# The first loads of a convolution's input on another queue, a longer pause behind them, and new shares for its stages

## The chip, the cores and the metric

The kernel runs on one core of a Trainium2 chip. The metric is device time in microseconds (us) of one execution, smaller is better; the time given for a kernel is the median of its runs. A core has five engines that each work through a queue of their own in order: TensorE (PE, matrix products; PEld is its loading of weights), VectorE (DVE), ScalarE (ACT), GpSimd (POOL) and SyncE (SP). SP computes nothing here: it issues DMAs. ACT and POOL can issue DMAs too, and an instruction of theirs that stands behind a DMA issue waits for that issue. Engines wait for each other by semaphores.

## The reference

Two branches over a sequence of S = 2048 rows of D = 576 numbers are summed with the input. Branch A is a short causal convolution of `k` (four taps), a product with `v`, a long causal convolution per channel (by FFT in the reference), and a gate. Branch B is a dense network with a ReLU.

```python
xn = _layernorm(x, axis=-1)
# A, with q = xn:
for t in range(ks):                                   # ks = 4
    k_shift = k_shift + k_pad[:, t:t + S, :] * shift_k[:, ks - 1 - t][None, None, :]
kv = k_shift * v
y = irfft(rfft(kv) * rfft(ssm_k)) + kv * ssm_D
A = q * y
# B:
B = maximum(xn @ w1, 0) @ w2                          # w1: 576 x 4608, w2: 4608 x 576
return x + A + B
```

## The kernel before

**Precision.** Matrix products are done with operands split into a high and a low part; a product is the sum of three: high by high, high by low, low by high. ACT makes the high part by a copy, DVE or POOL the low part by a subtraction.

**The network (FFN).** Its 4608 hidden columns are worked in 18 pairs of 2 x 128, and rows in four blocks of 512, two blocks a half: first half (blocks 0 and 1) over all 18 pairs, then second half (blocks 2 and 3), which uses a product scheme with fewer multiplications (`quad`, L515). A visit is one pair with one block. `mm1` (L539) makes two tiles `psh` of hidden values in PSUM, fourteen matmuls each. `relu` then has ACT write the high part `hh` (L521) and DVE the low part `ll` (L522). A `unit` (L602) multiplies `hh` and `ll` with a half of `w2`, twelve matmuls for two pairs, into a tile `pso`, which DVE adds to the accumulator `acc` (L606 or L610). There are three buffers for `pso` and two banks for `psh`. Weights come by SP (`load_w1`, L421 and L423; `load_w2`, L430) and are split by ACT (L439, L501) and POOL (L410).

**The long convolution.** `conv` is a generator of small steps that are strewn among the FFN's. Its stages: FK transforms the kernel `ssm_k` (matmuls L652, stores `zk` L718); FX makes the four taps, the product with `v` and the transform of the result (matmuls L652, stores `zx` L809); FM does the middle transform, the product with FK's result and the middle inverse (matmuls L848, loads `zk` and `zx`, stores `zy`); FO does the last inverse transform, gates and adds (matmuls L989, L990). In FX, `load(t)` (L733) loads a tile of `k` and of `v`, for t below 0 the shifted rows of `k` (L744, L745), all through `move` (L156) or directly; `sk` holds the four taps' factors (L729), each broadcast to 128 partitions. `tap` (L754, L757, L758) and `gate` (L763) are DVE's; `split` (L773, L776, L777) stacks the halves, and two DMAs on SP move a half of the result, `c`, into each stack `xs` (L780), on which the transform's matmuls work.

**Rows of the second half.** A second generator, `later_xT`, prepares the blocks 2 and 3 beside all this: it loads rows, normalizes them, stores them to DRAM as `nrm` (L325), loads them back in pieces, `rows` from `nrm` (L333), transposes (L338), splits, and stores the operands (`kept_t` L349, `kept_xr` L394).

**What sets the order.** The FFN's code calls `tick(cost)` with the columns of each few matmuls. `tick` adds `rate * cost` to a balance and lets `conv` take its next step when the balance is not negative. A step that yields a positive number costs that many units (`W_FK`, `W_FX`, `W_FM`, `W_FO`, with `N_...` steps each). A step that yields a negative number holds the stream until that many columns of the FFN have passed; `PAUSE` is 16,000 columns. `rate` is set so that the whole stream, `FFT_TOTAL` units and `PAUSES` pauses, fits into `SHARE` of the FFN's columns. A scheduler then puts the recorded instructions into each engine's queue; `here()` keeps a step's instructions behind the FFN's latest ones. The wait of a DMA on one of eight rotating semaphores keeps some eight DMAs of these two queues under way at a time.

```python
rate = FFT_TOTAL / (SHARE * FFN_TOTAL - PAUSES * PAUSE - START)
```

Of the kernel before, what the change touches and what calls it, by code (L numbers as in the profile page):

```python
# [17 lines left out]
P = 128  # L18
S = 2048
D = 576  # L20
# [3 lines left out]
NH = D // 2  # L24
# [24 lines left out]
PAUSE = 16000  # L49
# [2 lines left out]


N_FK, N_FX, N_FM, N_FO = 4 * T, 4 * T, 6 * NG, 4 * T
W_FK, W_FX, W_FM, W_FO = 1.25, 4.8, 1.72, 2.15
Q = 32
KB = 3
KT_GAP = 2000
PAUSES = 4 * NH // Q // KB * KT_GAP / PAUSE + 11
FFT_TOTAL = N_FK * W_FK + N_FX * W_FX + N_FM * W_FM + N_FO * W_FO  # L60
W_QUAD = sum(W_STAGE)
FFN_TOTAL = NPAIR * HB * (W_PLAIN + W_QUAD + 2 * 4 * W_UNIT)
# [47 lines left out]
def h3_ffn_kernel(ctx: ExitStack, tc, x, k, v, shift_k, ssm_k, ssm_D, w1, w2, fwd, inv, mid, out):  # L110
    nc = tc.nc
# [37 lines left out]
    def halves(u):  # L149

        return slice(u * A1, (u + 1) * A1), slice((1 - u) * A1, (2 - u) * A1)

    def move(tile_, rows, t, store=False, queues=(nc.sync, nc.sync)):
        for u in range(U):
            a, b = tile_[halves(u)[0]], rows[u, :, t]
            queues[u].dma_start(*((b, a) if store else (a, b)))  # L156
# [41 lines left out]
    def f32(t):  # L198
        return t.bitcast(F32)
# [437 lines left out]
    def load_const(pool, src, name):  # L637
        w = pool.tile([P, 2, P], F32R, tag="wt", name=name, bufs=3)
        nc.gpsimd.dma_start(w, src)
        return w  # L640
# [7 lines left out]
    def first(w, stk, z, u):  # L648

        ps = fft_psum()  # L650
        for n in range(2):
            nc.tensor.matmul(ps[:, :NH], w[:, n, :], stk, start=n == 0, stop=n == 1)  # L652
        nc.scalar.activation(z, ps[:, :NH], AF.Copy)  # L653

    @contextmanager
    def here():


        with tc.issue_after(done["acc"].ins), tc.issue_after(done["act"].ins):
            yield  # L660

    def conv():
# [4 lines left out]
        with tc.tile_pool(name="fk", bufs=2) as fp:  # L667
# [44 lines left out]
            for n, t2 in enumerate(order):  # L712
                stk, nxt = nxt, []
                u, t = divmod(t2, T)
# [11 lines left out]
        with tc.tile_pool(name="fx", bufs=2) as fp:  # L726
            sk = fp.tile([P, KS, D], F32, tag="sk", name="sk", bufs=1)
            for j in range(KS):
                nc.scalar.dma_start(sk[:, j, :], shift_k[j:j + 1, :].to_broadcast([P, D]))  # L729
            win, gates, mats, sums, stks = {}, {}, {}, {}, {}  # L730

            def load(t):
                win[t] = fp.tile([P, D], F32, tag="k", name=f"k{t}", bufs=KS + 1)  # L733
                queue = nc.scalar if t < 2 else nc.sync
                if t >= 0:
                    move(win[t], k, t, queues=(queue, queue))
                    gates[t] = fp.tile([P, D], F32, tag="v", name=f"v{t}")
                    move(gates[t], v, t, queues=(queue, queue))
                    if t == 0:
                        for n in range(3):  # L740
                            mats[n] = load_const(fp, fwd[n // U][:, n % U], f"wx{n}")
                else:
                    nc.vector.memset(win[t][0:1, :], 0.0)
                    queue.dma_start(win[t][1:A1, :], k[1, 0:A1 - 1, T + t, :])  # L744
                    queue.dma_start(win[t][A1:, :], k[0, :, T + t, :])  # L745

            def tap(t, n):

                if t >= T:
                    return  # L750
                with here():
                    if n == 0:
                        sums[t] = fp.tile([P, D], F32, tag="c", name=f"c{t}")
                        nc.vector.tensor_tensor(sums[t], win[t], sk[:, 0, :], OP.mult)  # L754
                    else:
                        e = fp.tile([P, D], F32, tag="e", name=f"e{t}_{n}")
                        nc.vector.tensor_tensor(e, win[t - n], sk[:, n, :], OP.mult)  # L757
                        nc.vector.tensor_tensor(sums[t], sums[t], e, OP.add)  # L758

            def gate(t):  # L760
                if t < T:
                    with here():
                        nc.vector.tensor_tensor(sums[t], sums[t], gates[t], OP.mult)  # L763

            def split(t):

                if t < T:
                    hi = fp.tile([P, D], F32R, tag="e", name=f"h{t}")
                    lo = sums[t].bitcast(F32R)
                    for u in range(U):  # L770
                        stks[t, u] = fp.tile([P, D], F32R, tag="stk", name=f"xs{t}_{u}", bufs=3)
                    with here():
                        nc.scalar.activation(hi, sums[t], AF.Copy)  # L773
                        for u in range(U):
                            own = halves(u)[0]
                            nc.scalar.activation(stks[t, u][own], sums[t][own], AF.Copy)  # L776
                        nc.vector.tensor_tensor(lo, sums[t], hi, OP.subtract)  # L777
                    for u in range(U):
                        own, other = halves(u)
                        nc.sync.dma_start(f32(stks[t, u])[other], sums[t][own])  # L780

            with here():
                for t in (0, *range(-1, -KS, -1), 1):
                    load(t)
            yield -3 * PAUSE
            for n in range(KS):
                tap(0, n)
                yield -PAUSE / 8
            gate(0)
            yield -PAUSE / 8  # L790
            split(0)
            yield -PAUSE / 8
            for n in range(KS):
                tap(1, n)
                yield -PAUSE / 4
            for t in range(T):
                if t + 2 < T:
                    load(t + 2)

                side = (((gate, t + 1),), ((split, t + 1),),  # L800
                        (), ((tap, t + 2, 0),),
                        ((tap, t + 2, 1),), (),
                        ((tap, t + 2, 2),), ((tap, t + 2, 3),))
                for u in range(U):
                    for h in range(2):
                        cols = slice(h * NH, (h + 1) * NH)
                        z = fp.tile([P, NH], F32, tag="z", name=f"zx_{t}_{u}_{h}", bufs=3)
                        first(mats[U * t + u], stks[t, u][:, cols], z, u)
                        nc.sync.dma_start(zx[:, T * u + t, cols], z)  # L809
                        for part in range(2):  # L810
                            for what, *args in side[4 * u + 2 * h + part]:
                                what(*args)
                            yield W_FX / 2
                    n = U * t + u + 3
                    if n < U * T:
                        mats[n] = load_const(fp, fwd[n // U][:, n % U], f"wx{n}")
# [186 lines left out]


    stream = conv()
    clock = {"ffn": 0.0, "conv": 0.0, "until": START, "done": False}
    rate = FFT_TOTAL / (SHARE * FFN_TOTAL - PAUSES * PAUSE - START)

# [161 lines left out]
```

## Time and profile before

| | us |
|---|---|
| median of 3 runs (lowest, highest) | 1087.82 (1085.5, 1089.77) |
| the profiled execution's own time | 1086.3 |
| its span, first to last instruction | 1084.5 |
| mean granted TensorE clock | 0.992 of full |
| DVE busy | 745.1 |
| ACT busy | 549.2 |
| POOL busy | 392.5 |
| DMA, mean rate | 189 GB/s |

The span is what all views count from: 0 is the first instruction. Busy times of different engines overlap. The views used are windows (busy time of each engine in a stretch of the span), the timeline (instructions in order, with the idle time before one and what ended it in brackets), the waits (who waited for whom, in total, how often, longest) and the rows of the page. In timelines, ACTq and SPq are the issuing of DMAs by ACT and SP. Buffer numbers are left out there, so `hh` stands for every `hh` tile.

### The profile page before, as it was taken

The page shows a single profiled execution, that of the slowest core. Times are in us where ns is not written, and L with a number is a line of the kernel's source. Part 1 is how long each engine was busy: PE and PEld are TensorE (multiplying, and loading weights), DVE is VectorE, ACT ScalarE, POOL GpSimd, SP SyncE. Part 2 cuts the span into 40 slices and gives each one's busy share as a digit, 9 for nine tenths or more (in the row PEclk, how much of TensorE's full clock was granted, in tenths as well). Part 3 has the DMA queues.
Part 4 walks back from the last instruction along what each step waited for, and adds up shares of the span by engine and source line. Part 5 has one row for each costly group of instructions (what it writes and reads, how often), then busy time and mean ns, then how long its engine had stood idle before and what let it go on. Part 6 is the DMA issues. An engine that isn't in the chain of part 4 may idle for free.

```text
span 1084.5 us, 19961 instructions
## 1 busy us (share of the span) xinstructions
PE 1058.6 (98%) x7145; PEld 992.8 (92%) x7145; DVE 745.1 (69%) x1310; ACT 549.2 (51%) x1201; POOL 392.5 (36%) x395
## 2 busy tenths in 40 slices
PE   8999999979899999999999999999999999999998
PEld 5799999969799999999899999999999999999998
DVE  5438788768787866652387677677767876576664
ACT  4225565524444333332567577776776765444431
POOL 4122333313323333333334334344433444444551
PEclk9999999989999999999999999999999999999999
DMA  7665776577886685444878455555555644997854
GB/s 194 142 158 175 184 208 197 166 204 202 229 241 192 189 266 150 126 116 148 274 217 242 148 170 166 167 179 156 165 155 157 189 136 131 320 304 235 259 174 110
DMA packets 156303, 204.45 MB, mean 189 GB/s; under 512 B 32845, under 2 KB 122703, under 8 KB 155180
## 3 DMA queue, kind: packets, MB, share of 16 engines
q1 hardware_dynamic: 141636, 185.76, 58.0%
q0 software_dynamic: 12576, 13.44, 5.2%
q10 hardware_dynamic: 1992, 3.98, 1.4%
q8 instruction: 56, 0.92, 0.4%
q14 instruction: 43, 0.35, 0.1%
HBM read 133.92 MB, written 55.05 MB: 174 GB/s over the span
## 4 chain that ended last, share of the span: by engine, by line
PE 88%; DMA 6%; DVE 2%; issue 1%; ACT 1%; POOL 0%; ACTq 0%; SPq 0%; POOLq 0%; DVEq 0%
PE pso L602 39%; PE psh L539 20%; PE psb L515 12%; PE psf L848 7%; PE psa L515 6%; PE psf L652 3%; DMA r<-in_w 3%; DMA ztk<-zk 1%; DMA zo<-zy 1%; PE psf L989 1%; PE psf L990 1%; DMA zy<-vo 1%; DMA xs<-c 1%; DMA k<-in_k 0%; DVE acc L606 0%
## 5 line engine op out<-in xcount | busy, mean ns | idle before, releaser
L602 PE MATMUL pso<-w,hh 128*128 128x288 f32 x2304 | 469.5, 296 | 6.1 <-ACT hh L521 4.7
L602 PEld LDWEIGHTS pso<-w,hh 128*128 128x128 f32 x2304 | 373.4, 188 | 15.1 <-ACT hh L521 5.8
L602 PE MATMUL pso<-w,ll 128*128 128x288 f32 x1152 | 329.0, 296 | 2.8 <-DVE ll L522 2.8
L410 POOL TENSOR_TENSOR g<-r,g 128x256 fp32r<-128x256 f32 (+2 forms) x145 | 163.3, 1132 | 397.8 <-ACT g L439 348.7
L539 PE MATMUL psh<-b,g 128*128 128x512 f32 x864 | 221.9, 400 | 0.5 <-ACT b L219 0.5
L602 PEld LDWEIGHTS pso<-w,ll 128*128 128x128 f32 x1152 | 213.0, 188 | 4.3 <-DVE ll L522 3.4
L539 PEld LDWEIGHTS psh<-b,g 128*128 128x128 f32 x864 | 159.8, 191 | 32.0 <-ACT b L219 1.0
L610 DVE TENSOR_TENSOR acc<-pso,acc 128x288 f32<-128x288 f32 x224 | 98.7, 450 | 74.9 <-PE pso L602 73.9
L410 POOL TENSOR_TENSOR w<-r,w 128x576 fp32r<-128x576 f32 x72 | 117.6, 1633 | 58.5 <-ACT w L501 58.4
L521 ACT ACTIVATE hh<-psh 128x512 fp32r<-128x512 f32 x72 | 42.9, 596 | 132.2 <-PE psh L539 115.2
L522 DVE SCALAR_TENSOR_TENSOR ll<-psh,hh 128x512 fp32r<-128x512 f32 x72 | 49.2, 684 | 73.6 <-ACT hh L521 73.5
L439 ACT ACTIVATE g<-r 128x256 fp32r<-128x256 f32 (+2 forms) x145 | 76.7, 542 | 35.3 <-DMA r<-in_w 27.6
L515 PE MATMUL psb<-t,g 128*128 128x256 f32 x648 | 93.9, 280 | 0.3 <-DVE psa L570 0.3
L515 PEld LDWEIGHTS psb<-t,g 128*128 128x128 f32 x648 | 84.9, 188 | 0.8 <-DVE psa L570 0.5
L468 POOL TENSOR_TENSOR r<-r 128x256 f32<-128x256 f32 x72 | 59.5, 846 | 52.1 <-DMA r<-in_w 50.6
L515 PE MATMUL psa<-b,g 128*128 128x256 f32 x432 | 62.7, 281 | 0.3 <-ACT psa L566 0.3
L515 PE MATMUL psb<-b,g 128*128 128x256 f32 x432 | 57.5, 281 | 0.0
L515 PEld LDWEIGHTS psa<-b,g 128*128 128x128 f32 x432 | 56.4, 188 | 0.5 <-ACT psa L566 0.5
L515 PEld LDWEIGHTS psb<-b,g 128*128 128x128 f32 x432 | 54.3, 188 | 0.0
L606 DVE SCALAR_TENSOR_TENSOR acc<-pso,rstd,acc 128x288 f32<-128x288 f32 x80 | 40.5, 511 | 18.9 <-PE pso L602 18.3
L839 DVE TENSOR_TENSOR lok<-ztk,hik 128x576 fp32r<-128x576 f32 x32 | 35.3, 1105 | 19.9 <-ACT hik L838 19.6
L653 ACT ACTIVATE zx<-psf 128x288 f32<-128x288 f32 x64 | 25.2, 405 | 46.4 <-issue 19.4
(137 smaller groups left out, 1665.9 us busy)
## 6 DMA issues: line engine op xcount, KB each, us to landing
r<-in_w SPq DMA_DIRECT2D x72, 288.0 KB, 4.0
zy<-vo SPq DMA_DIRECT2D x64, 288.0 KB, 3.3
zo<-zy SPq DMA_DIRECT2D x32, 576.0 KB, 5.9
r<-in_w SPq DMA_DIRECT2D x35, 512.0 KB, 4.8
zk<-zk SPq DMA_DIRECT2D x64, 144.0 KB, 2.2
zx<-zx SPq DMA_DIRECT2D x64, 144.0 KB, 2.6
ztk<-zk SPq DMA_DIRECT2D x32, 288.0 KB, 4.1
ztx<-zx SPq DMA_DIRECT2D x32, 288.0 KB, 3.1
```

The lines of the kernel that those rows point to most:

```text
L410: return nc.gpsimd.tensor_tensor(dst, src, hi, OP.subtract)
L439: nc.scalar.activation(hi, src, AF.Copy)
L468: nc.gpsimd.tensor_tensor(dst, a, b, op)
L515: nc.tensor.matmul(ps, a, m, start=start and i == 0, stop=i == len(seq) - 1, skip_group_check=not start)
L521: done["act"] = nc.scalar.activation(hh, ps, AF.Relu)
L522: lows.append(nc.vector.scalar_tensor_tensor(ll, ps, 0.0, hh, op0=OP.max, op1=OP.subtract))
L539: nc.tensor.matmul(ps, a, m, start=i == 0, stop=i == len(seq) - 1)
L602: nc.tensor.matmul(ps[:, :NH], a, m, start=c == 0, stop=c == len(seq) - 1)
L606: done["acc"] = nc.vector.scalar_tensor_tensor(acc[t][:, dc], ps[:, :NH], rstd[:, t:t + 1], acc[t][:, dc], op0=OP.mult, op1=OP.add)
L610: done["acc"] = nc.vector.tensor_tensor(acc[t][:, dc], ps[:, :NH], acc[t][:, dc], OP.add)
L839: nc.vector.tensor_tensor(lo, raw[name, g], hi, OP.subtract)
L848: nc.tensor.matmul(ps[:, :NH], a, m[:, cols], start=n == 0, stop=n == 2)
```

## The change

Two edits are in the code of stage FX. The sources of the first loads (`sk`, and `load` of tiles 0, −1, −2, −3 and 1) go to SP's queue, where they had gone to ACT's. The pause behind these loads is five units and was three, and the one behind each of the first tile's four taps is a quarter of a unit and was an eighth. Three numbers of the pacing follow: `PAUSES` grows by 2.5, the weight of a step of FM falls from 1.72 to 1.58, that of FO rises from 2.15 to 2.35.

```diff
-W_FK, W_FX, W_FM, W_FO = 1.25, 4.8, 1.72, 2.15
+W_FK, W_FX, W_FM, W_FO = 1.25, 4.8, 1.58, 2.35
-PAUSES = 4 * NH // Q // KB * KT_GAP / PAUSE + 11
+PAUSES = 4 * NH // Q // KB * KT_GAP / PAUSE + 13.5
             for j in range(KS):
-                nc.scalar.dma_start(sk[:, j, :], shift_k[j:j + 1, :].to_broadcast([P, D]))
+                nc.sync.dma_start(sk[:, j, :], shift_k[j:j + 1, :].to_broadcast([P, D]))
...
-                queue = nc.scalar if t < 2 else nc.sync
+                queue = nc.sync
...
                 for t in (0, *range(-1, -KS, -1), 1):
                     load(t)
-            yield -3 * PAUSE
+            yield -5 * PAUSE
             for n in range(KS):
                 tap(0, n)
-                yield -PAUSE / 8
+                yield -PAUSE / 4
```

The numbers move instructions on all engines from here on. Three places matter.

**The start of FX, on ACT and SP.** Names carry the tile's numbers: `hh7_1_1` is of pair 7, block 1, second tile. ACT before, from the first load of the factors on:

```order
L729 DMA sk_2156<-in_shift_k 128x576 x4
L156 DMA k0_2161<-in_k 64x576 x2
L156 DMA v0_2164<-in_v 64x576 x2
L744 DMA k-1_2173<-in_k 63x576
L745 DMA k-1_2173<-in_k 64x576
L744 DMA k-2_2177<-in_k 63x576
L745 DMA k-2_2177<-in_k 64x576
L744 DMA k-3_2181<-in_k 63x576
L745 DMA k-3_2181<-in_k 64x576
L156 DMA k1_2185<-in_k 64x576 x2
L156 DMA v1_2188<-in_v 64x576 x2
L521 ACTIVATE hh7_1_1_2640<-psh7_1_1_2625 128x512
```

ACT at the same place now, from the instruction on that stood just ahead of these:

```order
L347 ACTIVATE area2_680<-area2_680 128x256
L521 ACTIVATE hh7_1_1_2622<-psh7_1_1_2607 128x512
L392 ACTIVATE rows2_679<-rows2_679 64x512
L521 ACTIVATE hh7_0_0_2677<-psh7_0_0_2661 128x512
L439 ACTIVATE g8_1_2704<-r1_8_2518 128x512
```

SP before, behind the last store of FK:

```order
L718 DMA zk_86<-zk31_1_2140 128x288
L349 DMA kept_t_92<-area2_680 128x2x256
L430 DMA r2_8_0_2602<-in_w2 128x2x288
L156 DMA k2_2714<-in_k 64x576 x2
L394 DMA kept_xr_93<-rows2_679 128x512
L430 DMA r2_8_1_2734<-in_w2 128x2x288
```

SP now, behind the same store:

```order
L729 DMA sk_2156<-in_shift_k 128x576 x4
L156 DMA k0_2161<-in_k 64x576 x2
L156 DMA v0_2164<-in_v 64x576 x2
L744 DMA k-1_2173<-in_k 63x576
L745 DMA k-1_2173<-in_k 64x576
L744 DMA k-2_2177<-in_k 63x576
L745 DMA k-2_2177<-in_k 64x576
L744 DMA k-3_2181<-in_k 63x576
L745 DMA k-3_2181<-in_k 64x576
L156 DMA k1_2185<-in_k 64x576 x2
L156 DMA v1_2188<-in_v 64x576 x2
L430 DMA r2_8_0_2584<-in_w2 128x2x288
```

The 18 loads left ACT; on SP they stand ahead of the weights `r2_8_0` and of the store `kept_t`, which had no load ahead of them.

**The first taps, on DVE.** Before, from the first tap's product `c0` on:

```order
L754 TENSOR_TENSOR c0_2396<-k0_2161,sk_2156 128x576
L757 TENSOR_TENSOR e0_1_2422<-k-1_2173,sk_2156 128x576
L757 TENSOR_TENSOR e0_2_2441<-k-2_2177,sk_2156 128x576
L758 TENSOR_TENSOR c0_2396<-c0_2396,e0_1_2422 128x576
L758 TENSOR_TENSOR c0_2396<-c0_2396,e0_2_2441 128x576
L757 TENSOR_TENSOR e0_3_2479<-k-3_2181,sk_2156 128x576
L754 TENSOR_TENSOR c1_2576<-k1_2185,sk_2156 128x576
L522 SCALAR_TENSOR_TENSOR ll7_1_1_2641<-psh7_1_1_2625,hh7_1_1_2640 128x512
L393 TENSOR_TENSOR rows2_679<-rows2_679 64x512
L522 SCALAR_TENSOR_TENSOR ll7_0_0_2698<-psh7_0_0_2679,hh7_0_0_2697 128x512
L758 TENSOR_TENSOR c0_2396<-c0_2396,e0_3_2479 128x576
L610 TENSOR_TENSOR acc4_222<-pso6_4_0_2701,acc4_222 128x288
```

DVE now, from the low part `ll7_1_1` on:

```order
L522 SCALAR_TENSOR_TENSOR ll7_1_1_2623<-psh7_1_1_2607,hh7_1_1_2622 128x512
L606 SCALAR_TENSOR_TENSOR acc2_99<-pso5_2_1_2626,rstd_84,acc2_99 128x288
L338 STREAM_TRANSPOSE rows2_679<-rows2_679 64x512
L606 SCALAR_TENSOR_TENSOR acc2_99<-pso5_3_1_2647,rstd_84,acc2_99 128x288
L754 TENSOR_TENSOR c0_2533<-k0_2161,sk_2156 128x576
L393 TENSOR_TENSOR rows2_679<-rows2_679 64x512
L757 TENSOR_TENSOR e0_1_2557<-k-1_2173,sk_2156 128x576
L757 TENSOR_TENSOR e0_2_2603<-k-2_2177,sk_2156 128x576
L758 TENSOR_TENSOR c0_2533<-c0_2533,e0_1_2557 128x576
L522 SCALAR_TENSOR_TENSOR ll7_0_0_2678<-psh7_0_0_2661,hh7_0_0_2677 128x512
L610 TENSOR_TENSOR acc4_222<-pso6_4_0_2681,acc4_222 128x288
```

`ll7_1_1` moved from behind the second tile's first tap to ahead of all taps; `ll7_0_0` and the eviction of `pso6_4_0` moved ahead of the second add, of `e0_3` and of the second tile's first tap.

**The fourth tile of FX, on SP.** Before, the rows around the stacks `xs3`:

```order
L333 DMA rows3_2736<-nrm_88 32x16x32 x2
L780 DMA xs3_0_3020<-c3_2916 64x576
L780 DMA xs3_1_3021<-c3_2916 64x576
L809 DMA zx_85<-zx_2_1_1_3090 128x288
L430 DMA r2_10_0_3292<-in_w2 128x2x288
L333 DMA rows3_2736<-nrm_88 32x16x32 x6
```

SP now, up to the same stacks:

```order
L333 DMA rows3_2712<-nrm_88 32x16x32 x7
L430 DMA r2_10_0_3228<-in_w2 128x2x288
L809 DMA zx_85<-zx_2_0_0_3153 128x288
L809 DMA zx_85<-zx_2_0_1_3185 128x288
L809 DMA zx_85<-zx_2_1_0_3212 128x288
L333 DMA rows3_2712<-nrm_88 32x16x32
L780 DMA xs3_0_3170<-c3_3072 64x576
L780 DMA xs3_1_3171<-c3_3072 64x576
```

The eight loads of `rows` from `nrm` all stand ahead of `xs3` now; six of them stood behind it. Further on, FM's steps stand closer to each other among the FFN's instructions, and FO's less close.

## The prediction

> **What bounds the kernel now.** The page first: who is busy, and what the chain that ended last is made of.
>
> ```profile
> PE 1058.6 (98%) x7145; PEld 992.8 (92%) x7145; DVE 745.1 (69%) x1310; ACT 549.2 (51%) x1201; POOL 392.5 (36%) x395
> PE 88%; DMA 6%; DVE 2%; issue 1%; ACT 1%; POOL 0%; ACTq 0%; SPq 0%; POOLq 0%; DVEq 0%
> ```
>
> TensorE sets the time: it is busy for 98% and makes up 88% of the chain. The change leaves its 7145 matmuls alone, so only two things can move the time: places where PE stands idle, and places where it runs at a lowered clock. Windows of 20 us find both. A row's columns are the length, then busy time and (count) of PE, PEld, DVE, ACT and POOL, then granted clock, DMA share and GB/s.
>
> ```profile
> 220.00:240.00 20.00, 13.50 (x66) 11.63 (x65) 11.82 (x17) 2.68 (x5) 3.13 (x2) 0.79 0.74 208
> 240.00:260.00 20.00, 20.00 (x114) 17.88 (x113) 18.05 (x39) 8.59 (x17) 5.35 (x5) 0.96 0.84 230
> ...
> 280.00:300.00 20.00, 16.80 (x90) 14.59 (x89) 13.94 (x19) 6.96 (x14) 7.94 (x7) 0.91 0.84 213
> 300.00:320.00 20.00, 20.00 (x121) 18.15 (x121) 17.62 (x31) 10.65 (x22) 4.61 (x6) 1.00 0.88 233
> ...
> 520.00:540.00 20.00, 18.55 (x137) 17.77 (x135) 6.72 (x12) 10.05 (x23) 7.82 (x9) 1.00 0.92 296
> ...
> 560.00:580.00 20.00, 19.40 (x144) 18.33 (x143) 13.93 (x27) 11.40 (x27) 5.08 (x5) 1.00 0.94 281
> 580.00:600.00 20.00, 19.57 (x149) 19.16 (x150) 15.57 (x27) 15.66 (x36) 9.76 (x9) 1.00 0.71 216
> ...
> 940.00:960.00 20.00, 18.08 (x136) 17.41 (x135) 14.86 (x27) 9.01 (x21) 10.61 (x12) 1.00 1.07 315
> ```
>
> 300:320 is the healthy state. Four places differ. **A**, 220 to 260: 20 − 13.50 = 6.5 us idle, plus slow running of 0.21 × 13.50 = 2.8 and 0.04 × 20 = 0.8, together **10.1 us**. **B**, 280 to 300: 3.2 idle plus 0.09 × 16.80 = 1.5, **4.7 us**. **C**, 520 to 600: 1.45 + 0.60 + 0.43, **2.5 us**. **D**, 940 to 960: **1.9 us**. A is the largest, and its cause stands in ACT's timeline (ACTq is ACT's own issuing of DMAs):
>
> ```profile
> 214.18 0.42 ACT L347 ACTIVATE area<-area 128x256 fp32r<-128x256 f32 x1 [0.82 <-DVE area L387]
> 215.28 2.02 ACTq L729 DMA_DIRECT2D sk<-in_shift_k  x4
> 217.33 1.44 ACTq L156 DMA_DIRECT2D k<-in_k  x2
> 219.23 3.42 ACTq L156 DMA_DIRECT2D v<-in_v  x2
> 222.69 0.75 ACTq L744 DMA_DIRECT2D k-1_2173<-in_k  x1
> 226.27 0.47 ACTq L745 DMA_DIRECT2D k-1_2173<-in_k  x1
> ...
> 230.21 1.25 ACTq L156 DMA_DIRECT2D v<-in_v  x2
> 231.51 0.60 ACT L521 ACTIVATE hh<-psh 128x512 fp32r<-128x512 f32 x1 [16.91 <-DMA k-3_2181<-in_k]
> ```
>
> From 214.6 to 231.5 ACT computes nothing: it issues the first loads of the conv input, and some of those issues wait. The eviction `hh7_1_1` (L521) stands behind them. PE's timeline shows the price:
>
> ```profile
> 220.93 2.95 PE L539 MATMUL psh<-b,g 128*128 128x512 f32 x12
> ...
> 227.63 0.30 PE L602 MATMUL pso<-w,ll 128*128 128x288 f32 x1
> 232.16 1.81 PE L602 MATMUL pso<-w,hh 128*128 128x288 f32 x6 [4.24 <-ACT hh L521]
> 236.24 0.85 PE L602 MATMUL pso<-w,ll 128*128 128x288 f32 x2 [2.26 <-DVE ll L522]
> 236.88 5.16 PE L539 MATMUL psh<-b,g 128*128 128x512 f32 x12
> ```
>
> PE runs out of `hh` at 227.9, waits 4.24 us, then 2.26 us more for the `ll` made from it; after that the same twelve matmuls take 5.16 us instead of 2.95. In the sum, A is idle time and lowered clock alike.
>
> **The change, part by part.** *Loads from ACT to SP* (4 + 2 + 2 + 6 + 2 + 2 = 18 DMAs). ACT loses all 18; `hh7_1_1` then stands next behind L347, as the order shows, and can run when its matmuls end. Term: **−10.1 us**. What takes its place: SP now holds the 18, and DVE still needs their data. Three DVE rows say when the data came:
>
> ```profile
> 227.58 0.76 DVE L754 TENSOR_TENSOR c<-k,sk 128x576 f32<-128x576 f32 x1 [5.93 <-DMA k<-in_k]
> 229.05 0.76 DVE L757 TENSOR_TENSOR e<-k-1_2173,sk 128x576 f32<-128x576 f32 x1 [0.70 <-DMA k-1_2173<-in_k]
> 230.22 0.76 DVE L757 TENSOR_TENSOR e<-k-2_2177,sk 128x576 f32<-128x576 f32 x1 [0.42 <-DMA k-2_2177<-in_k]
> ```
>
> In the new order `ll7_1_1` stands ahead of the taps, but `ll7_0_0` and the eviction of `pso6_4_0` still stand behind `e0_2`. There are three `pso` buffers, so `pso6_7_0` needs that eviction. I date its need from PE's undisturbed pace:
>
> ```profile
> 314.20 3.25 PE psh L539 x14
> 317.72 3.18 PE pso L602 x24
> ```
>
> `psh7_0_0` ends at about 224.2 (twelve matmuls from 220.93 and two more); two units take 3.2, `psh7_0_1` 3.25, `pso6_6_0` 1.6: the buffer is needed at 232.2. By the old landing, `e0_2` ends at 231.0; one add (0.75), `ll` (0.7) and the eviction (0.45) end near 232.9, which is 0.7 late. But two DMAs that ran beside the loads now stand behind them on SP:
>
> ```profile
> r<-in_w SPq DMA_DIRECT2D x72, 288.0 KB, 4.0
> kept_t<-area SPq DMA_DIRECT2D x12, 256.0 KB, 2.8
> ```
>
> These 544 KB (557,000 bytes), at the 208 GB/s of 220:240, are 2.7 us, so the data may come up to that much sooner. Between no wait and, if landing slips as far the other way (0.7 + 2.7), 3.4 us, I take **+1.0**, nearer the row. Other work behind SP's 18: the weights `r2_8_0`, `kept_t`, `kept_xr`, the loads of `rows3` and of `r1_9`. In the row 216.21 below the weights started early; by the order their split `w2_8_0` comes only after `g9_0`. That split ran at 248, so without A's 10 us it is due near 238; issued behind the 18 loads near 231 and landing 4.0 later, the weights come 3 us ahead of it: **0**. If that cover goes, PE pays up to one such load, 4.0 us.
>
> ```profile
> 216.21 0.43 SPq L430 DMA_DIRECT2D r<-in_w  x1
> 248.27 0.67 ACT L501 ACTIVATE w<-r 128x576 fp32r<-128x576 f32 x1
> ```
>
> *Longer pause, spread taps* (5 for 3, a quarter for an eighth, +2.5 units of 16,000 columns). They add no instruction and make no engine wait; they move taps behind FFN evictions. The stage ahead of the conv transforms starts later in the order, and this moves C away from the change of halves. C is 2.5; half of it may go, all of it, or it may double: **−1.0**, from −2.5 to +2.5.
>
> *B stays.* Its rows:
>
> ```profile
> 283.99 1.30 SPq L333 DMA_DIRECT2D rows<-nrm  x2
> 285.40 1.21 SPq L780 DMA_DIRECT2D xs<-c  x2
> ...
> 287.79 4.01 SPq L333 DMA_DIRECT2D rows<-nrm  x6
> ...
> 294.40 1.14 SPq L780 DMA_DIRECT2D xs<-c  x2
> PE psf L652 <- DMA xs<-c: 3.2, 2, 2.7
> ```
>
> PE's 3.2 us are waits for `xs`, whose DMAs stand on SP among eight `rows<-nrm`. In the new order all eight stand ahead of `xs3`, where two did. The collision is moved by one tile, not removed: **0**, from −4.7 (it slips into slack) to +4.0 (the six DMAs that came behind are now ahead).
>
> The trace has the longest idle of B at 2.7 us and still a granted clock of 0.91. The Trainium skill, page "TensorE: Matmul & The Clock Gate", section "Part 1: The HAM clock gate", has the clock halve after at least one idle window of about 3.4 us; the trace disagrees here, since 2.7 us were enough. By the page's figures A would be worth 6.5 idle plus one window at half speed, an estimate of 8.2 instead of 10.1, and the time 1079.6.
>
> *Shares* (FM 1.72 to 1.58, FO 2.15 to 2.35, pauses 12.5 to 15). The code's rate goes from 855.04 / 1,701,057 to 840.96 / 1,661,057 a column. FM then lasts 599,000 columns instead of 657,000 (9% less), FO 23,000 more, pauses 40,000 more, FK and FX 5,500 less: the sum is zero, and the stream ends where it ended. FM's density is covered by idle engines:
>
> ```profile
> 600.00:900.00 300.00, 299.96 (x2291) 296.02 (x2291) 221.85 (x381) 210.39 (x469) 119.91 (x106) 1.00 0.54 160
> ```
>
> Even 10% more of everything there leaves DVE at 244 and ACT at 231 of 300 us, so **0**; if the cover went, the price is that of the third rival. D: FO starts sooner and runs thinner, **0**, from −1.0 to +3.0.
>
> **Sum:** −10.1 + 1.0 − 1.0 + 0 + 0 = −10.1. The profiled execution took 1086.3 us (span 1084.5 and 1.8 around it), hence 1076.2; the median of the runs lies 1.5 above that execution: **1077.7 us**.
>
> **Rivals.** *First, the wait moves on to DVE and SP.* For it: DVE's 5.93 us wait for `k` and the 0.7 us worked out above, and 18 DMAs of SP at some 0.5 us each with the same waits. Against it: of what PE needs within 8 us of 224, only that eviction stands behind the taps. Its price is the 3.4 us bound, with the clock lost again (as 2.8 + 0.8 in A) and half of a weight load, 2.0: 9.0 back instead of 1.0, and the time is 1085.7. In the same direction, the Trainium skill, page "DMA: Bandwidth & Descriptors", section "Issuing engines are not separate DMA queues", says that DMAs of any issuer share 16 DMA engines and another issuer saves only issue time. By that the data comes no sooner; ACT's freedom is what is won, and the trace agrees in so far as the issuing of 18 loads alone held ACT's queue for 16 us.
>
> *Second, B and C go too*, because the taps now run ahead of their need: −10.1 + 1.0 − 4.7 − 2.5, which gives 1071.5. For it: B's waits are few, 3.2 us in two. Against it: the eight `rows<-nrm`.
>
> *Third, slower:* FM's density breaks its cover. FM has 32 groups; each step hands from ACT to DVE to PE, and a group that misses its turn holds PE. The point where it decides is 10.1 / 32 = 0.32 us a group. PE's rows of this stage, first start to last, give its length:
>
> ```profile
> L848 PE MATMUL psf<-hik,m_sb x128: 288/295/301, 527.1 to 889.2; 128*128 128x288 f32 x128
> L848 PE MATMUL psf<-yh,m_sb x128: 288/294/301, 550.7 to 914.5; 128*128 128x288 f32 x128
> ```
>
> That is 387 us, or 353 with 9% off, 17 windows of 20 us. At the 1.45 us that 520:540 lost they cost 24.6, and the time is 1102.3. Against it: 0.04 us idle in the 300 us above.
>
> **How the numbers follow.** Forecast 0.66 (own range 1073 to 1083), second rival 0.12, first 0.17, third 0.05. The range 1071 to 1085 leaves out the third, most of the first's far side, and little else. A measurement of this kernel tells about 0.5% (5.4 us) from no change. Faster by more needs less than 1082.4: nearly all of the forecast and second, and a fifth of the first, 0.80; within: 0.15; slower: the third, 0.05.
>
> **What would show it.** Right: no ACT gap near 214 to 231 in the new trace; `hh7_1_1` within a microsecond of its matmuls; PE busy 19 or more of 20 in 220:240 at clock 1.00; the 18 issues as SPq rows of some 15 us. B near 270 to 290 with waits for `xs`. Wrong: PE waiting for DVE `acc` or `ll` at 230 to 240; PE waiting for weights at 245; new small idles spread over FM.

## The result, and the profile after

| | before | after |
|---|---|---|
| median of the runs, us | 1088.8 (1085.5 to 1091.55, 4 runs) | 1078.57 (1074.42 to 1079.81, 4 runs) |
| ratio, 95% interval | | 0.9913 (0.9889 to 0.9938) |
| span of the profiled execution, us | 1084.5 | 1078.0 |

Faster by 0.9%, more than the half per cent that can be told from no change. The medians differ by 10.2 us, the two profiled executions by 6.5. A second measurement of the same kernel (`a1_after` below) gave a ratio of 0.9941 (0.9922 to 0.996), so the gain is better read as 6.5 to 9.5 us, the two ratios' range, than as 10.2.

The page of the kernel after, who is busy and what the chain that ended last is made of:

```profile
PE 1055.2 (98%) x7145; PEld 993.1 (92%) x7145; DVE 744.5 (69%) x1310; ACT 550.0 (51%) x1201; POOL 394.1 (37%) x395
PE 82%; DMA 7%; DVE 5%; ACT 3%; issue 2%; SPq 1%; POOL 0%; DVEq 0%; ACTq 0%; POOLq 0%
```

PE still sets the time, and its 7145 matmuls are the same. Windows of 20 us of the kernel after, with the columns of the prediction's (length, busy time and count of PE, PEld, DVE, ACT, POOL, granted clock, DMA share, GB/s):

```profile
220.00:240.00 20.00, 19.87 (x119) 17.79 (x118) 14.00 (x23) 5.45 (x10) 3.96 (x3) 1.00 0.92 254
240.00:260.00 20.00, 16.68 (x93) 15.10 (x93) 17.74 (x38) 7.14 (x15) 4.80 (x5) 0.91 0.77 200
...
280.00:300.00 20.00, 18.00 (x111) 16.27 (x110) 17.02 (x29) 8.32 (x19) 5.30 (x6) 1.00 0.88 225
...
580.00:600.00 20.00, 19.51 (x148) 18.75 (x147) 14.55 (x25) 15.09 (x36) 6.99 (x8) 1.00 0.60 181
...
900.00:920.00 20.00, 17.33 (x123) 16.90 (x123) 7.53 (x16) 5.99 (x13) 8.98 (x11) 0.91 1.04 306
```

Read them as before: idle time of PE, plus (1 − clock) times its busy time. 220 to 240 is healthy. A new place stands 20 us on, called **A'** here: 3.32 idle + 0.09 × 16.68 = 4.8 us. B is down to 2.0. Of C only 0.5 is left; 520 to 580 has PE at 20.00 of 20. D has moved to 900 to 920 and grown: 2.67 + 0.09 × 17.33 = 4.2. So between before and after, A went from 9.3 to 0.1, A' from 0.8 to 4.8, B from 4.7 to 2.0, C from 2.5 to 0.5 and D from 1.9 to 4.2: 19.2 became 11.7. Of those 7.5 us some 2 go back at 0 to 40 us, which no edit touches and which differs from execution to execution (the window 20:40 has a granted clock of 0.91 here and in `e2_pauses`, and 1.00 before and in `e1_queue`). That leaves 5.5, about a microsecond less than the difference of the spans (6.5).

ACT's timeline after, at the old gap:

```profile
215.65 0.42 ACT L347 ACTIVATE area<-area 128x256 fp32r<-128x256 f32 x1 [0.81 <-DVE area L387]
219.26 0.60 ACT L521 ACTIVATE hh<-psh 128x512 fp32r<-128x512 f32 x1 [3.19 <-PE psh L539]
```

The 16.91 us gap is gone: the eviction `hh` now waits for its own matmuls only. PE's waits after, longest first (in all, times, longest):

```profile
PE psf L652 <- DMA v<-in_v: 3.3, 1, 3.3
PE psf L652 <- DMA xs<-c: 2.7, 2, 2.0
PE psf L989 <- DMA wi<-in_inv: 2.7, 1, 2.7
```

Before, the list was led by ACT's `hh`, 4.7 us. Now its three longest are all transfers. The first is the wait at A'. Its releaser is inferred as `v`, but L652 reads only the halves `xs` and the weights `wx`, and it began as the halves of the first tile landed (issued from 243.24 on, 4.9 us each from issue to landing). The same goes for the L652 rows further below, whatever releaser they name. SP's timeline after, ahead of them:

```profile
216.79 1.76 SPq L729 DMA_DIRECT2D sk<-in_shift_k  x4
...
229.86 1.24 SPq L156 DMA_DIRECT2D v<-in_v  x2
231.20 0.53 SPq L430 DMA_DIRECT2D r<-in_w  x1
...
236.90 2.38 SPq L156 DMA_DIRECT2D rows<-in_x  x4
239.33 0.58 SPq L421 DMA_DIRECT2D r<-in_w  x1
239.95 1.15 SPq L423 DMA_DIRECT2D r<-in_w  x2
243.24 1.14 SPq L780 DMA_DIRECT2D xs<-c  x2
```

The 18 first loads hold SP from 216.8 to 231.1. In the 6 us ahead of `xs` stand four `rows` loads of 288 KB and `r1_9` (one of 512, two of 64 KB): 1.8 MB. DVE's and PE's timelines after, at the same place:

```profile
242.09 0.46 DVE L172 BATCH_NORM_STATS2 bn<-rows 128x6 f32<-128x288 f32 x1 [2.15 <-DMA rows<-in_x]
242.47 0.74 DVE L777 TENSOR_TENSOR c<-c,h 128x576 fp32r<-128x576 f32 x1
```

```profile
248.69 0.51 PE L652 MATMUL psf<-xs,wx 128*128 128x288 f32 x2 [3.32 <-DMA v<-in_v]
```

Three explanations offer themselves: the halves are issued late, because the split L777 stands behind a statistics instruction that waits 2.15 us for `rows`; SP's queue is full ahead of them; or the DMA engines (share 0.92 in the window 220:240) still have 1.8 MB to move. They can hold together; the experiments bear on each.

### The profile page after: what moved, and what is told of

The parts are those of the page before. It is cut to its first block, busy times and chain, and to the rows that moved or that the text cites. A ratio compares the mean times of both kernels' runs of the same rounds, so it can differ in the third digit from the quotient of the medians.

```text
span 1078.0 us, 19964 instructions
## 1 busy us (share of the span) xinstructions
PE 1055.2 (98%) x7145; PEld 993.1 (92%) x7145; DVE 744.5 (69%) x1310; ACT 550.0 (51%) x1201; POOL 394.1 (37%) x395
## 4 chain that ended last, share of the span: by engine, by line
PE 82%; DMA 7%; DVE 5%; ACT 3%; issue 2%; SPq 1%; POOL 0%; DVEq 0%; ACTq 0%; POOLq 0%
PE pso L602 37%; PE psh L539 18%; PE psb L515 11%; PE psf L848 6%; PE psa L515 5%; PE psf L652 3%; DMA xs<-c 2%; DMA r<-in_w 1%; DMA wi<-in_inv 1%; DMA sk<-in_shift_k 1%; PE psf L989 1%; DMA zo<-zy 1%; PE psf L990 1%; DVE yl L873 1%; DMA k<-k 0%
## 5 line engine op out<-in xcount | busy, mean ns | idle before, releaser
L602 PE MATMUL pso<-w,hh 128*128 128x288 f32 x2304 | 470.4, 296 | 1.9 <-DVE acc L606 1.4
L602 PEld LDWEIGHTS pso<-w,hh 128*128 128x128 f32 x2304 | 374.4, 189 | 10.0 <-DVE acc L606 1.6
L602 PE MATMUL pso<-w,ll 128*128 128x288 f32 x1152 | 328.5, 296 | 0.5 <-DVE ll L522 0.5
L410 POOL TENSOR_TENSOR g<-r,g 128x256 fp32r<-128x256 f32 (+2 forms) x145 | 167.9, 1164 | 404.1 <-ACT g L439 353.6
L539 PE MATMUL psh<-b,g 128*128 128x512 f32 x864 | 218.0, 395 | 0.8 <-ACT b L219 0.5
L602 PEld LDWEIGHTS pso<-w,ll 128*128 128x128 f32 x1152 | 213.6, 189 | 1.5 <-DVE ll L522 0.7
L539 PEld LDWEIGHTS psh<-b,g 128*128 128x128 f32 x864 | 156.9, 188 | 31.3 <-ACT b L219 1.0
L610 DVE TENSOR_TENSOR acc<-pso,acc 128x288 f32<-128x288 f32 x224 | 98.5, 450 | 72.1 <-PE pso L602 70.9
L410 POOL TENSOR_TENSOR w<-r,w 128x576 fp32r<-128x576 f32 x72 | 115.3, 1602 | 57.2 <-ACT w L501 57.0
L515 PE MATMUL psb<-t,g 128*128 128x256 f32 x648 | 96.5, 281 | 0.4 <-DVE psa L570 0.4
L521 ACT ACTIVATE hh<-psa 128x512 fp32r<-128x512 f32 x36 | 21.5, 598 | 62.1 <-PE psa L515 61.8
L891 DVE TENSOR_TENSOR k<-psf,k 128x288 f32<-128x288 f32 x64 | 29.0, 454 | 34.0 <-ACT sw L890 33.1
```

Source lines behind the costliest of these rows:

```text
L410: return nc.gpsimd.tensor_tensor(dst, src, hi, OP.subtract)
L515: nc.tensor.matmul(ps, a, m, start=start and i == 0, stop=i == len(seq) - 1, skip_group_check=not start)
L521: done["act"] = nc.scalar.activation(hh, ps, AF.Relu)
L539: nc.tensor.matmul(ps, a, m, start=i == 0, stop=i == len(seq) - 1)
L602: nc.tensor.matmul(ps[:, :NH], a, m, start=c == 0, stop=c == len(seq) - 1)
L610: done["acc"] = nc.vector.tensor_tensor(acc[t][:, dc], ps[:, :NH], acc[t][:, dc], OP.add)
```

## The experiments

Each kernel was measured beside the kernel before on the same chip: one chip for the first four, one for the next four, one for the last two. The table works out PE's loss (idle plus lowered clock, from windows of 20 us as above) at each place, from one profiled execution of each kernel. The two rows of the kernel after (`after` and `a1_after`) differ by up to 2.1 us at one place, so smaller differences between rows say little. The expectations below give some of these losses a little higher (5.6 for B before, 5.1 for A' after, 4.5 for D after); the text goes by the table.

| kernel | median, us | ratio to before (95%) | A 220–240 | A' 240–280 | B 280–300 | C 520–600 | D 900–960 |
|---|---|---|---|---|---|---|---|
| before | 1085 to 1086 | 1 | 9.3 | 0.8 | 4.7 | 2.5 | 1.9 |
| after (first) | 1078.57 | 0.9913 (0.9889–0.9938) | 0.1 | 4.8 | 2.0 | 0.5 | 4.2 |
| e1_queue | 1081.64 | 0.9962 (0.9947–0.9976) | 0.1 | 8.4 | 2.0 | 4.1 | 2.2 |
| e2_pauses | 1080.25 | 0.9959 (0.9946–0.9972) | 7.4 | 0.0 | 1.9 | 0.4 | 2.3 |
| e3_shares | 1082.03 | 0.9974 (0.9961–0.9988) | 9.9 | 0.8 | 5.0 | 0.0 | 0.9 |
| e4_slack | 1079.61 | 0.9942 (0.992–0.9964) | 0.0 | 3.9 | 1.1 | 6.8 | 4.8 |
| a1_after | 1078.5 | 0.9941 (0.9922–0.996) | 0.1 | 5.0 | 4.1 | 1.1 | 4.1 |
| e5_queue_pauses | 1076.86 | 0.9923 (0.9902–0.9943) | 0.2 | 5.0 | 2.2 | 1.0 | 4.7 |
| e7_xs_pool | 1079.05 | 0.9948 (0.9929–0.9967) | 0.1 | 7.2 | 1.9 | 0.5 | 1.3 |
| e9_inverse_start | 1075.78 | 0.9915 (0.9894–0.9936) | 0.1 | 4.9 | 1.1 | 0.5 | 1.0 |
| e11_rows_2 | 1072.39 | 0.9878 (0.9858–0.9898) | 0.1 | 1.3 | 2.0 | 0.7 | 2.5 |
| e12_rows_3 | 1071.74 | 0.9871 (0.9846–0.9897) | 0.1 | 2.1 | 0.0 | 0.5 | 3.7 |

(Before was 1088.8 beside the first after, 1085.59 beside the first four experiments, 1084.99 beside the next four, 1086.24 beside the last two; ratios are what to compare across rows.)

### The parts alone

**e1_queue: the queue alone**, on the kernel before.

```diff
-                nc.scalar.dma_start(sk[:, j, :], ...)
+                nc.sync.dma_start(sk[:, j, :], ...)
-                queue = nc.scalar if t < 2 else nc.sync
+                queue = nc.sync
```

> Only the queue of the first loads is changed; pauses and shares are those of before. Theory (what held PE at 228 to 240 was ACT standing in DMA issues): ACT has no gap of 16 us any more, the 6.5 us idle and the lowered clock of 220 to 260 go, but the first transform, which stands early in PE's order, waits for its stack xs, 4 to 6 us with some clock lost, since the stack's DMAs come behind 18 loads and the row loads on SP. C and D stay at 2.5 and 1.9. Net -3 to -7 us against before. Rival 1 (the pause, not the queue, is the cure: DVE stands in the taps ahead of ll): PE waits for DVE ll or acc at 230 to 240 for 5 us or more, net 0 to -2. Rival 2 (the shares bring the gain): net 0.

It took 4.1 us off by the ratio, as expected. Two windows of `e1_queue`, then its SP row of the first halves and the PE row that waits for them:

```profile
220.00:240.00 20.00, 19.89 (x119) 17.82 (x118) 14.05 (x24) 6.46 (x11) 4.71 (x4) 1.00 0.91 244
240.00:260.00 20.00, 13.94 (x71) 12.11 (x70) 16.15 (x36) 5.90 (x12) 3.07 (x4) 0.83 0.73 191
```

```profile
239.97 1.18 SPq L780 DMA_DIRECT2D xs<-c  x2
```

```profile
247.66 1.78 PE L652 MATMUL psf<-xs,wx 128*128 128x288 f32 x6 [6.06 <-DMA k<-in_k]
```

A goes by this edit alone, and 8.4 us come back at A', with the short pause. C, expected to stay, grew from 2.5 to 4.1. The halves are issued here at 239.97, and PE begins at 247.66. This stretch runs 1.9 us earlier here than in the kernel after (the first tile's gate, L763, starts at 235.00 instead of 236.88). Counted from the gate, the halves are issued 1.4 us sooner than there, yet PE begins 0.85 us later. So a sooner issue alone doesn't help.

**e2_pauses: the pauses alone**, on the kernel before.

```diff
-PAUSES = ... + 11
+PAUSES = ... + 13.5
-            yield -3 * PAUSE
+            yield -5 * PAUSE
                 tap(0, n)
-                yield -PAUSE / 8
+                yield -PAUSE / 4
```

> Only the pauses are changed (5 for 3, a quarter for an eighth, 2.5 units more in the sum); the loads stay on ACT's queue and the shares are those of before. Theory: ACT's gap of 16 us stays and PE waits for hh (4 us) and ll, 6 to 10 us with the clock, as before; what may move are B and C. Net 0 to -4 us. Rival 1: DVE no longer stands in front of ll, PE's wait falls to under 3 us, net -7 or more. Rival 2: net 0.

It took 4.5 us off by the ratio, a little more than the 0 to 4 expected. The window and the wait of `e2_pauses` at A:

```profile
220.00:240.00 20.00, 15.21 (x77) 13.36 (x76) 10.54 (x16) 2.69 (x5) 3.33 (x2) 0.83 0.81 220
```

```profile
PE pso L602 <- ACT hh L521: 4.5, 3, 4.0
```

ACT's gap is still there, so A stays at 7.4. The gain is B (4.7 to 1.9) and C (2.5 to 0.4), with 1.9 of A and 0.8 of A'.

**e3_shares: the shares alone**, on the kernel before.

```diff
-W_FK, W_FX, W_FM, W_FO = 1.25, 4.8, 1.72, 2.15
+W_FK, W_FX, W_FM, W_FO = 1.25, 4.8, 1.58, 2.35
```

> Only the weights of FM (1.58 for 1.72) and FO (2.35 for 2.15) are changed; queue and pauses are those of before. Theory: A and B stay as before (10.1 and 4.7 us), C and D change by up to 2 us each with opposite signs, net -2 to +2 us. Rival 2: C's gain is the shares', net -4 or more. Rival 1: net 0.

It took 2.8 us off by the ratio. The expectation missed: C and D were to change with opposite signs, −2 to +2 in all, and both fell. The windows from 520 to 600 us of `e3_shares` all have PE at 20.00 of 20, so C's 2.5 us are gone; FM's denser steps cost little (0.44 us idle in 600 to 900, where before had 0.04).

**e4_slack: one more unit of pause**, on the kernel after, behind the second tile's taps.

```diff
-PAUSES = ... + 13.5
+PAUSES = ... + 14.5
                 tap(1, n)
-                yield -PAUSE / 4
+                yield -PAUSE / 2
```

> The changed kernel with one unit of pause more between the first tile's split and its first transform (behind each of the second tile's four taps half a unit for a quarter, 14.5 for 13.5 in the sum). Theory (in the changed kernel PE's 3.3 us at 245 to 249 and the lowered clock behind it come of a transform that stands in PE's order before its stack has landed): the wait goes, 240 to 260 is 19.5 or more of 20 at clock 1.00, -3 to -5 us against the changed kernel, a ratio to before near 0.987. Rival (the DMA queue is so full there that the wait moves along with the transform): the wait stays at 2 us or more, 0 to -1 us against the changed kernel.

No gain, where 3 to 5 us were expected: 0.9942, where the kernel after has 0.9941 in `a1_after` below. The wait for the first halves went (PE's idle time in 240:260 is 0.41), but a wait of 1.89 for the second tile's came at 267.75, and at 540 to 580 this row and window of `e4_slack`:

```profile
PE psf L848 <- DVE k L891: 3.9, 1, 3.9
```

```profile
560.00:580.00 20.00, 16.90 (x109) 16.77 (x110) 14.54 (x25) 14.83 (x33) 6.84 (x6) 0.83 0.53 146
```

The unit shifted every later stage too. PE's wait at 563 leads back to a transfer. The instruction it waits for, L891, stood on VectorE behind L839; that had waited 4.64 us for ScalarE's L838, which had waited 4.65 us for the load of `ztk` from `zk` (5.5 us from issue to landing). More slack was no cure here: in this execution it was paid for elsewhere, at a place that neither the theory nor the rival had.

### The whole again, and without the shares

**a1_after** is the kernel after, unchanged.

> The changed kernel itself, beside its parts on one chip. Measured alone, the queue edit took 4.1 us off, the pauses 4.5 and the shares 2.8, each against the same runs of the kernel before. If the three parts took away different stalls, the whole is worth their sum, 11.4 us, a ratio of 0.9895. If they share stalls, it is worth less: the queue edit and the pauses each took 3 of the 5.6 us that PE loses at 280 to 300 us, which can be won only once, and the whole alone loses 4.5 us at 900 to 960 us, so that 11.4 - 3 - 2 = 6 to 7 us are left, a ratio of 0.994.

The ratio is 0.9941: 6.5 us, the lower of the two sums. The parts don't add up (11.4), because the queue and the pauses each win B, the pauses and the shares each win C, and D is larger in the whole (4.2 and 4.1) than in any part (0.9 to 2.3).

**e5_queue_pauses** is the kernel after with the old shares (the first line of `e3_shares`' diff taken back).

> The changed kernel with the old shares. Theory: the shares moved the start of the inverse stage from 921 to 903 us, to a place where PE waits 2.7 us for its first weights, and are otherwise worth nothing on top of the pauses, which clear the stall at 520 to 600 us already; then without them PE loses no more than before at 900 to 960 us (2.0 to 2.8 instead of 4.5), the place at 240 to 260 us stays at about 5, and the time is that of the changed kernel or up to 2 us below it. Rival: the shares' own 2.8 us add up with the rest; then this is 2 to 3 us slower than the changed kernel.

The time came out 1.6 us below the whole, as the theory had it, but the interval is as wide as that. Its reason was wrong: D is as large (4.7) without the shares, and only waits for another transfer. The wait and the window of `e5_queue_pauses`:

```profile
PE psf L989 <- DMA zo<-zy: 3.2, 2, 2.7
```

```profile
920.00:940.00 20.00, 17.29 (x119) 16.80 (x120) 9.59 (x19) 8.07 (x20) 6.26 (x8) 0.91 1.09 322
```

So on top of the pauses the shares are worth nothing that can be measured, and D can be as large without them.

### What holds A' and D

**e7_xs_pool**: the kernel after, with the first tile's halves issued by POOL.

```diff
-                        nc.sync.dma_start(f32(stks[t, u])[other], sums[t][own])
+                        (nc.gpsimd if t < 1 else nc.sync).dma_start(
+                            f32(stks[t, u])[other], sums[t][own])
```

> The changed kernel, with the two transfers of the first tile's halves (xs) issued by GpSimd instead of SyncE. Theory: PE's 3.3 us at 245 to 249 us are those two transfers standing behind 1.8 MB (four rows loads, r and two r loads) that SyncE has issued in the 6 us before; from GpSimd's queue they land in under 3 us instead of 5, the wait is under 1 us and PE loses under 2 us at 240 to 260 us instead of 5.1: 3 to 4 us faster than the changed kernel, unless the later loads lose it again. First rival: all queues share the 16 DMA engines, which are full there (0.92 of them at 220 to 240 us); the halves land as late as now and nothing is won, within 1 us. Second rival: the split on VectorE (L777), which stands behind a statistics instruction that waits 2.15 us for the rows, sets the time; then the issue stays at 243 us, the landing after it at about 5 us, and nothing is won.

Nothing won. POOL's and PE's rows of `e7_xs_pool`:

```profile
241.63 1.09 POOL L780 DMA_DIRECT2D xs<-c  x2 [9.75 <-DVE c L777]
```

```profile
248.00 0.82 PE L652 MATMUL psf<-xs,wx 128*128 128x288 f32 x2 [4.63 <-issue]
```

POOL had waited for nothing but the split, and SP's queue no longer stood ahead; the halves still took 5.9 us to land (4.9 from SP, in the kernel after). So SP's queue, the theory, isn't the cause. The run doesn't part the two rivals: counted from the gate the split ran no sooner (5.7 us behind it, 5.6 in the kernel after) and the issue neither (6.7 and 6.4), as the second has it, and the landing was no shorter, as the first has it. The Trainium skill, page "DMA: Bandwidth & Descriptors", section "Issuing engines are not separate DMA queues", says that DMAs run on the same 16 engines whichever engine starts them. The trace agrees as far as it goes: the landing isn't shorter from POOL.

**e9_inverse_start**: the kernel after, with less asked for at the start of FO.

```diff
-            for n in range(3):
+            for n in range(2):
                 load_z(n)
-            for i in range(2):
-                load_rest(i)
+            load_rest(0)
             yield -PAUSE
+            load_z(2)
+            load_rest(1)
```

> The changed kernel with less loaded ahead of the inverse stage's first matmul: two spectra blocks and one tile's weights and rows before the pause, the third block and the second tile's behind it. Theory: the 2.7 us of PE at 909 to 912 us are the first weights standing among 2.7 MB that were all asked for within 5 us; with some 1.6 MB ahead they land 2 to 3 us sooner, and PE loses 1.5 to 2.5 us at 900 to 920 us instead of 4.5: 2 to 3 us faster than the changed kernel. Rival: the bytes are only put off, and PE waits as long for the third block or the second weights, 8 us later; then nothing is won, within 1 us, and the loss stands at 920 to 940 us.

Its median is 2.7 us below that of `a1_after`, as expected, but the intervals of the two overlap. The windows of `e9_inverse_start`, and PE's wait for the first weights `wi` there:

```profile
900.00:920.00 20.00, 19.71 (x147) 18.84 (x146) 11.52 (x24) 8.65 (x20) 9.64 (x12) 1.00 1.04 308
920.00:940.00 20.00, 19.26 (x149) 18.88 (x148) 11.54 (x24) 9.68 (x23) 9.65 (x12) 1.00 1.07 314
```

```profile
PE psf L990 <- DMA wi<-in_inv: 0.2, 1, 0.2
```

The DMA engines are as full as before (share 1.04), and PE hardly waits. But the edit isn't shown to be what did that. `e12_rows_3` below has it too, and waits for the same weights:

```profile
PE psf L990 <- DMA wi<-in_inv: 2.1, 1, 2.1
```

And `e7_xs_pool`, without the edit, waits only 0.8 us for them.

**e11_rows_2 and e12_rows_3**: on `e9_inverse_start`, the preparation of the last block of rows begins two or three of its steps later.

```diff
     def later_xT(b):
...
+        for _ in range(2 * (b == NB - 1)): yield    # 3 in e12_rows_3
         for i in range(0, BT, 2):
             with here():
                 nc.vector.memset(hold[:, i * D:i * D + 1], 0.0)
                 move(hold[...], x, ...)
```

> The kernel with the lighter inverse start (2.8 us faster than the changed kernel), and the feed-forward's last rows block asked for two steps later: of its four loads of 288 KB one is issued ahead of the first tile's halves (xs) and three behind them, where all four were ahead. Theory: PE's 3.4 us at 245 to 248 us are 1.8 MB that SyncE asked for ahead of the halves, which the DMA engines move at some 250 to 300 GB/s; without 0.86 MB of them the halves land 2.9 to 3.5 us sooner, the wait is under 1 us, and PE loses 0.5 to 2 us at 240 to 260 us instead of 5.2: 3 to 4 us faster than the kernel it starts from, a ratio to before near 0.988, unless the rows, now late, stop VectorE ahead of an eviction. Rival: the first taps, not the transfers, set the time (the split L777 waits for ScalarE's copies), and the halves are issued at 242 us and land at 248 us as before; then nothing is won, and the ratio stays near 0.9915.

> As the run before, three steps later: all four rows loads stand behind the halves. Theory: 1.15 MB less ahead of them, so they land 4 us sooner and PE waits nothing there; the loss at 240 to 260 us is under 1 us, 4 to 5 us less than 5.2, and this is 0 to 1 us faster than with two steps, unless the chain of the rows (statistics, transposes, kept operands), which now ends three steps later, is late for its reader at 500 to 530 us; then PE loses 1 to 4 us there. Rival as before: the loss at 240 to 260 us stays at 5.

Both ratios came out as the theory had them: 0.9878 and 0.9871 where 0.988 and 0 to 1 us less were expected. The waits didn't quite: 1.3 and 1.5 us at 240 to 260, where under 1 was expected of both. SP's timeline of `e11_rows_2`, then its PE row and window:

```profile
240.41 0.54 SPq L156 DMA_DIRECT2D rows<-in_x  x1
241.05 1.18 SPq L780 DMA_DIRECT2D xs<-c  x2
242.28 2.17 SPq L156 DMA_DIRECT2D rows<-in_x  x3
```

```profile
246.39 0.50 PE L652 MATMUL psf<-xs,wx 128*128 128x288 f32 x2 [1.33 <-ACT hh L521]
```

```profile
240.00:260.00 20.00, 18.67 (x112) 16.65 (x111) 18.68 (x34) 7.73 (x16) 7.50 (x7) 1.00 0.89 233
```

Three of the four `rows` loads stand behind the halves, and A' falls from 4.9 to 1.3. In `e12_rows_3` all four do; two windows of it:

```profile
240.00:260.00 20.00, 18.47 (x106) 16.06 (x106) 18.81 (x36) 9.74 (x18) 8.04 (x7) 1.00 0.97 248
...
280.00:300.00 20.00, 20.00 (x122) 18.38 (x123) 17.37 (x26) 8.22 (x17) 5.07 (x5) 1.00 0.82 234
```

The first halves aren't waited for at all; the 1.53 us of 240:260 are a wait for the second tile's, at 255, which the `rows` now stand ahead of. B is gone but for 0.6 us, which fall just ahead of 280; the `rows<-nrm` of this block come later too (from 286.7 instead of 272.7). The late reader at 500 to 530 us, feared in the expectation, doesn't show: 500 to 580 has PE at 20.00. D, though, is back at 3.7 in this execution. At 1071.74 us, 0.9871 (0.9846 to 0.9897), it has the lowest median here, 7.6 us faster than the kernel after by the two ratios ((0.9941 − 0.9871) × 1086), with the edit of `e9_inverse_start` in it. The intervals of the two rows kernels overlap each other, and just touch that of `e9_inverse_start`.

These two runs also take the statistics instruction (L172), which waits for the `rows`, away from ahead of the split L777. VectorE's rows of `e9_inverse_start`, then of `e11_rows_2`:

```profile
236.18 0.76 DVE L763 TENSOR_TENSOR c<-c,v 128x576 f32<-128x576 f32 x1
...
241.33 0.46 DVE L172 BATCH_NORM_STATS2 bn<-rows 128x6 f32<-128x288 f32 x1 [2.08 <-DMA rows<-in_x]
241.71 0.74 DVE L777 TENSOR_TENSOR c<-c,h 128x576 fp32r<-128x576 f32 x1
```

```profile
236.59 0.76 DVE L763 TENSOR_TENSOR c<-c,v 128x576 f32<-128x576 f32 x1
...
239.59 0.75 DVE L777 TENSOR_TENSOR c<-c,h 128x576 fp32r<-128x576 f32 x1
```

So there are two things to part, the place of the split and the bytes ahead of the halves. All times of this table are us; all but the landing are counted from the start of the gate L763:

| kernel | split L777 | halves issued | issue to landing | PE's first transform |
|---|---|---|---|---|
| before | 2.9 | 3.9 | 4.6 | 9.7, not waiting |
| after (first) | 5.6 | 6.4 | 4.9 | 11.8 |
| e1_queue | 3.7 | 5.0 | 6.9 | 12.7 |
| e7_xs_pool | 5.7 | 6.7 | 5.9 | 13.1 |
| e9_inverse_start | 5.5 | 6.3 | 5.1 | 12.0 |
| e11_rows_2 | 3.0 | 4.5 | 4.9 | 9.8 |
| e12_rows_3 | 3.0 | 3.8 | 4.3 | 8.5, not waiting |

`e1_queue` has the early split and all four `rows` loads ahead of the halves: they take 6.9 us to land, and PE starts no sooner than with the late split. `e11_rows_2` issues them about as early behind one of the four, and PE starts 2.9 us sooner. So the early split alone wins nothing (`e1_queue` also lacks the longer pause). But of the 2.2 us that `e11_rows_2` wins on `e9_inverse_start` here, 1.8 are the sooner issue and only some 0.3 a shorter time behind it. Moving the `rows` does both at once. Fewer bytes with the late split weren't tried, so the share of each stays open.

## Why the prediction was right, and where it wasn't

The forecast was 1077.7 us and 10.1 less than before; the medians gave 1078.57 and 10.2 less. That the two meet to 0.1 us is luck, as the second measurement (6.5 us) and the terms show. By places the first execution won 7.5 us: A' and D cost 3.0 and 2.3 more than their terms, B and C won 2.7 and 1.0 more.

- **A, −10.1: the mechanism is right.** ACT's gap, the wait for `hh` and the lowered clock are gone wherever the loads are on SP (0.0 to 0.2 at 220 to 240, from 9.3), and stay where they aren't (7.4 and 9.9 in `e2_pauses` and `e3_shares`). The other 0.8 of the 10.1 lie at 240 to 260, under A'.
- **"I take +1.0, nearer the row": wrong in place and size.** It was given to the eviction of `pso6_4_0` behind the taps. That costs nothing: DVE ran it (L610) at 233.31, and PE's idle time in 220:240 is 0.13. In its place 4.0 us came back at A' (4.8 against 0.8). Two things hold it. The step that failed is "Other work behind SP's 18", which named the loads of `rows3` and `r1_9` but gave only the weights `r2_8_0` a price. Their 1.8 MB collide with the first halves, because PE comes to these sooner: at 245.4 (248.69 − 3.32), 2.1 us behind their issue, where before it came 5.8 us behind it and waited for nothing (the last two rows of this list). The second thing, VectorE's order, has no term at all. The split ran 2.9 us behind the gate before and runs 5.6 behind it now, as a statistics instruction now stands ahead of it and waits 2.15 us for those `rows`. The first rival had it in kind, that a wait with its lowered clock comes back on transfers. Of the up to 2.7 us by which the data was to come sooner, 1.0 came: the first tap, which waits for `k0`, ran 11.3 us behind the first load's issue (228.08 − 216.79) instead of 12.3 (227.58 − 215.28).
- **C, −1.0: −2.0 (−1.4 in `a1_after`).** Pauses alone and shares alone each clear it, the queue alone doesn't (4.1), which fits the step, that the place of the later stages counts. Within its bounds.
- **B, 0: −2.7 in the first execution, −0.6 in the second.** The order was read rightly: all eight `rows<-nrm` do stand ahead of `xs3`. The inference from it failed, since seven of them had been issued before `xs3` could be. SP's and PE's rows after:

```profile
272.74 5.48 SPq L333 DMA_DIRECT2D rows<-nrm  x7
...
281.20 1.18 SPq L780 DMA_DIRECT2D xs<-c  x2
```

```profile
285.27 0.77 PE L652 MATMUL psf<-xs,wx 128*128 128x288 f32 x4 [2.00 <-DMA xs<-c]
```

They were through the queue at 278.2, and the split of this tile ran at 280.39, so `xs3` was issued 0.8 us behind it; before, the split ran at 279.11 and the issue at 285.40, 6.3 us behind. An instruction that stands ahead costs only what it still lacks when the next one is ready.

- **D, 0 with bounds −1.0 to +3.0: +2.3.** Within the bounds, which were set for the shares; but `e5_queue_pauses` loses 4.7 without them. What PE waits for there are early transfers of FO (`wi`, or `zo` in `e5_queue_pauses`). That the pile of loads makes them late is argued, not shown: asking for less left 1.0 in `e9_inverse_start`, but 2.5 and 3.7 in the two kernels built on it, and `e7_xs_pool` lost only 1.3 with the whole pile. Why it differs so stays open.
- **FM's density, 0: right.** The window of the kernel after for 600 to 900:

```profile
600.00:900.00 300.00, 299.83 (x2293) 296.12 (x2292) 230.25 (x399) 218.65 (x491) 124.31 (x106) 1.00 0.57 169
```

0.17 us idle in 300, with DVE up from 222 to 230. The slower rival falls; the second, that B and C go too, came out in part (−2.7 and −2.0 of its −4.7 and −2.5).

SP's and PE's rows of the first halves in the kernel before, for the second point:

```profile
243.33 1.18 SPq L780 DMA_DIRECT2D xs<-c  x2
```

```profile
249.16 0.95 PE L652 MATMUL psf<-xs,wx 128*128 128x288 f32 x6
```

## What to carry to other kernels

When a long stall goes, ask which transfers had been landing under cover of it: they now meet what PE needs next, and moving DMAs to a queue with time to spare frees the engine that issued them, and here brought the data only 1.0 us sooner. Look at two things ahead of each small transfer that PE waits for: the bytes asked for in the few microseconds before it, whichever queue asks, and what stands ahead of the instruction that makes its data, above all one that waits for those bytes. Putting large loads that nobody needs yet behind the transfer changed both, and won 4 to 5 us by the ratios (0.9915 to 0.9878 and 0.9871, intervals just touching); adding slack won nothing. Parts of a change that shift the same schedule can win the same stalls, so that their gains alone don't add up: 11.4 us here, where the whole was worth 6.5 to 9.5.

## What the runs showed of the hardware beyond that

How long an idle time lowers the clock was not one number. In the kernel after, 2.00 us of waiting at 285 left the granted clock of the window at 1.00, as 2.2 did in `e5_queue_pauses`; 2.67 us at 909 and 3.32 at 245 brought 0.91. But in `e4_slack` a wait of 1.89 us at 267.75 was enough: the window 260:280 has 0.91, and a pair of L602 matmuls took 0.68 us instead of 0.42 for some 3 us behind it. The Trainium skill, page "TensorE: Matmul & The Clock Gate", section "Part 1: The HAM clock gate", gives about 3.4 us of idling; the runs disagree, all of these being shorter. A wait of about 2 us may therefore cost nearly twice its length or no more than it. In two executions of the kernel after, B came to 2.0 and 4.1: the wait was 2.00 and 2.56 us, and the other 1.5 are the lowered clock (0.91 in the second).
